# wo loaded behind the last feed-forward weights, its low parts on VectorE, the first chunk's loads in written order, later x by the sync queue

## The chip, the cores and the metric

The kernel runs on one core of a Trainium2 chip. The metric is the device time of one execution in microseconds (us), as the median of several runs. The work is shared by TensorE (PE: matrix multiplications), VectorE (DVE), ScalarE (ACT), GpSimd (POOL) and the sync engine (SP), which only issues transfers (DMAs). ACT issues some transfers too. Each engine works through its own list of instructions in order, and an instruction that waits for another engine or for a transfer holds up all that stands behind it on its engine.

## What is computed

One sequence of 2048 tokens with 512 features. The layer-normalised input goes two ways: through an attention of 32 heads of 16 features, in which each token sees 8 earlier ones, two apart, and through a feed-forward net of 1792 hidden units with a squared ReLU. The result is the input plus the attention's output times the SiLU of the feed-forward's output.

```python
xn = _layernorm(x)
# attention
q, k, v = (xn @ wqkv) split into 32 heads of 16
idx = pos[:, None] - (arange(8) * 2)[None, :]      # masked where idx < 0
logits = einsum("bhsd,bhswd->bhsw", q, k[idx]) * 0.25
s = einsum("bhsw,bhswd->bhsd", softmax(logits), v[idx]) @ wo
# feed-forward
h = relu(xn @ w1 + b1) ** 2
g = silu(h @ w2 + b2)
return x + s * g
```

## The kernel before

**Number format.** Every matrix product is made of three passes: each float32 operand is split into a high part (a copy rounded to the format that TensorE reads, by `high`, on ACT) and a low part (what the rounding left, by `low`, a subtraction). `PASSES` multiplies high by high, high by low and low by high.

**Stages.** The tokens are 16 tiles of 128. The first stage normalises and transposes the tiles and makes q, k and v, which go to DRAM in head order (`sq`, `sk`, `sv`). The transposed tiles of later chunks are stored too (`sx`). The second stage is the feed-forward net and the output product, in four chunks `c` of 512 tokens. In each chunk the loop over `f`, the 14 blocks of 128 hidden units, calls `up(c, f)` (12 matmuls into a PSUM tile `ph`) and, two blocks behind, `down` (12 matmuls that add to four PSUM tiles `pb`). Blocks 0 and 1 of a chunk are computed at the end of the stage before it. `out_product(t)` multiplies tile t of the attention's output with `wot`, the split wo.

**ph and its two buffers.** The `ph` tiles share two PSUM buffers, so `up(0, f)` writes where `up(0, f - 2)` wrote. In chunk 0, for f from 2 to 11, ACT makes the ReLU, the high part of its square and the square itself, all out of `ph` and the last one back into `ph`, and `lowh(f)` on VectorE subtracts the high part: only then is the buffer free. For other f and in later chunks GpSimd subtracts from a copy in SBUF.

**Attention on VectorE.** The attention is a generator, `attention`, over 8 units of 256 tokens: per unit four times a product and a reduction for the logits (`pr`, then `L`), a softmax, and four times a product and a reduction for the output (`pv`, then `v`), which `store` writes to `so`. Its instructions are placed between the others by a planner: `clock` holds a running estimate of TensorE's and of VectorE's time, and `pump(margin)` emits attention work as long as VectorE's estimate stays below TensorE's plus the margin. `load` asks for k, q and v of a unit: `defer` holds the issue (by ACT) until TensorE's estimate has reached a due time, which is VectorE's estimate plus `FREE` (2000 ns). `start` notes when the data should be there (`LOAD`, 10500 ns later), and the planner places no work on it before.

**Weights.** `load_w(f)` loads a raw block of w1 and of w2 into two of four buffers (tag `z`), and `next_w` splits the next block (high on ACT, low on GpSimd) and asks for the block two further on. In the loop of chunk 0, step f splits block f + 3 and asks for block f + 5, so that step 8 asks for the last, block 13. wo is loaded raw at steps 3 and 6 (`rwo`, two tiles, four transfers of 32 partitions each) and split at steps 6 to 9, its low parts on GpSimd. `load_o` loads a unit of the attention's output (`oq`), `trans_o` transposes it on VectorE and copies the high part on ACT, `lowo` makes the low part, `load_r` loads rows of x for the residual, `finish` multiplies, adds and stores.

**Order.** Compute instructions keep the order in which the program writes them (`keep_in_program_order`). Of the transfers that SP issues, those through `queue` keep it among themselves; those through `dma` are put where a scheduler finds it best. The chunk's transposed x (`load_xT`, tile `xU`) is issued by ACT, behind `up(c, 13)` of the chunk before.

Of the kernel before, what the change touches and what calls it, by code (L numbers as in the profile page):

```python
# [9 lines left out]
F32 = mybir.dt.float32  # L10
# [5 lines left out]
P = 128  # L16
S = 2048
D = 512
# [15 lines left out]
BI = 16  # L34
# [18 lines left out]

MATMUL, VMATMUL, TRANSPOSE, DVE_FIXED, SHARED, SLACK, LATE, ROOM0, ROOM = 227, 120, 150, 150, 200, 500, 3000, 500, 3500

BEHIND, FAR, FREE, LAND, LOAD = 5000, 9000, 2000, 4500, 10500


@with_exitstack
def body(ctx: ExitStack, tc: tile.TileContext, x, wqkv, wo, w1, b1, w2, b2, out):  # L60
# [3 lines left out]
    clock = {"PE": 0.0, "V": 0.0}  # L64
# [30 lines left out]
    PE, V, A, G = Ordered(nc.tensor, "PE"), Ordered(nc.vector, "V"), Ordered(nc.scalar), Ordered(nc.gpsimd)  # L95
# [4 lines left out]
    dma = nc.sync.dma_start  # L100

    def queue(out, in_):

        tc.keep_in_program_order(dma(out, in_))
# [16 lines left out]
    def psT(name):  # L121
        return psum.tile([P, 512], F32, name=name, tag="tp", bufs=2)
# [4 lines left out]
    def high(hi, lo, src):  # L127
        A.activation(hi, src, AF.Copy)

    def low(hi, lo, src, eng):  # L130
        eng.tensor_sub(lo, src, hi.bitcast(F32))

    def split(hi, lo, src, eng):
        high(hi, lo, src)
        low(hi, lo, src, eng)
# [13 lines left out]
    def tile_rows(a, t):  # L149
        return a[t // 2 * UP:(t // 2 + 1) * UP, :].rearrange("(p e) d -> e p d", e=2)[t % 2]  # L150
# [109 lines left out]
    def attention():  # L260
# [74 lines left out]
        def store(u):  # L335
            v = tiles.pop(("v", u))
            row = so[0, u * UP:u * UP + 1, :]
            dst = bass.AP(tensor=row.tensor, offset=row.offset, ap=[[BI * CH, NB], [S * CH, GR], [1, BI * CH]])
            dma(dst, v[:, :BI, :].rearrange("p i c -> p (i c)"))
            done_units[0] = u + 1  # L340

        def load(u, names):
            if u == NU:
                return
            for n in names:
                while done_tiles[n][0] < 2 * (u + 1):
                    yield None
                t = max(clock["V"] + FREE if u else 0, done_tiles[n][1][u] + LAND)
                if u == 1 and n != "v" and n not in released:
                    held[n] = partial(start, n, u)  # L350
                else:
                    defer(t, partial(start, n, u))
# [47 lines left out]

    def load_w(f):
        r1, r2 = (piece(f"{n}{f}") for n in ("w1r", "w2r"))
        send = queue if f < 2 else dma
        send(r1.rearrange("p (k c) -> p k c", c=P), w1[:, f * P:(f + 1) * P].rearrange("(k p) c -> p k c", p=P))
        send(r2, w2[f * P:(f + 1) * P, :])
        raws[f] = r1, r2

    def next_w():
# [186 lines left out]
    def load_xT(c):  # L595
        xT[c] = xTa.tile([P, KT, TPC, 2, P], FR, name=f"xU{c}", tag="xT")
        for kt in range(KT):
            A.dma_start(xT[c][:, kt].bitcast(F32), sx[c][:, kt])

    hs = {}  # L600

# [21 lines left out]
    def lowh(f):  # L623
        h, ph, t = hs[f]
        if ph is not None:
            not_before(t)
            V.tensor_sub(h[:, 1], ph, h[:, 0].bitcast(F32))
# [282 lines left out]
    oqs, oTs = {}, {}  # L910

    def load_o(u, force):

        if u in oqs or (done_units[0] <= u and not force):
            return
        while done_units[0] <= u:
            flush(None)
            pump(clock["V"] - clock["PE"] + 4000)
        oqs[u] = p2.tile([P, UP // 64, 2, 2, CH], F32, name=f"oq{u}", tag="oq")
        for g in range(GR):  # L920
            src = so[g, u * UP:(u + 1) * UP, :].rearrange("(b p e) c -> p b (e c)", p=32, e=2)
            dma(oqs[u][32 * (g // 2):32 * (g // 2) + 32, :, g % 2].rearrange("p b e c -> p b (e c)"), src)

    def trans_o(t, pT):
        src = pT.rearrange("p (g n) -> p g n", g=4)
# [11 lines left out]
    def out_product(t, ps, cols=slice(0, D)):  # L937
        o = oTs[t]
        n = 0
        for g in range(4):  # L940
            for a, b in PASSES:
                PE.matmul(ps[:, cols], o[:, a, g], wot[:, b, g, cols], start=n == 0, stop=n == 11)
                n += 1
        pws[t] = ps
# [6 lines left out]

    def load_r(t):
        xrs[t] = p2.tile([P, D], F32, name=f"xr{t}", tag="xr", bufs=2)
        dma(xrs[t], tile_rows(x, t))

    def finish(t, eng, xt=None, cols=slice(0, D)):
        z = gs[t // TPC, t % TPC]
# [9 lines left out]
    for c in range(NCH):  # L967
        last = c == NCH - 1
        if c == 0:
            for j in range(TPC):  # L970
                begin(c, j)
        pb = [pbs[c, j] for j in range(TPC)]
        t0 = c * TPC
        room = ROOM if c else ROOM0
        for f in range(2, NF):
            up(c, f)
            if c == 0:
                next_w()
            pump()
            if c == 0 and f in (3, 6):  # L980

                i = f // 6
                rwo[i] = p2.tile([P, 2, D], F32, name=f"rwo{i}", tag="oT", bufs=2)
                for q in range(4):
                    rows = wo[q * P + 64 * i:q * P + 64 * i + 64, :].rearrange("(g p) n -> p g n", g=2)
                    dma(rwo[i][32 * q:32 * q + 32], rows)
            if c == 0:
                if 6 <= f < 10:
                    split(wot[:, 0, f - 6], wot[:, 1, f - 6], rwo[(f - 6) // 2][:, (f - 6) % 2], G)
            elif f == 2:  # L990
                finish(t0 - 4, G)
            elif f == 3:
                finish(t0 - 3, G)
                load_r(t0 - 2)
                load_r(t0 - 1)
                trans_o(t0 - 2, psT(f"pT{t0 - 2}"))
                trans_o(t0 - 1, psT(f"pT{t0 - 1}"))
            elif f == 4:
                lowo(t0 - 2)
                lowo(t0 - 1)  # L1000
            elif f == 5:
                out_product(t0 - 2, psT(f"pw{t0 - 2}"))
            elif f == 6:
                finish(t0 - 2, G)
                out_product(t0 - 1, psT(f"pw{t0 - 1}"))
            elif f == 7:
                finish(t0 - 1, G)
            if f == 2 and c:
                load_o(c * 2 - 1, True)
            elif f >= 7:  # L1010
                load_o(c * 2, f >= 9)
            if f in (9, 10) and not last:
                load_r(t0 + f - 9)
            if f == 10:
                for i in range(2):
                    trans_o(t0 + i, psT(f"pT{t0 + i}"))
            if f == 11:
                for i in range(2):
                    lowo(t0 + i)
            if f == 11 or (last and f > 11):  # L1020
                load_o(c * 2 + 1, f > 12)
            downs = [f - 2]
            if last and f == NF - 1:
                downs = []
            elif not last and f > NF - 3:
                downs = [f - 3, f - 2] if f == NF - 1 else []
            for i in downs:
                for j in range(TPC):
                    down(pb, i, j)
            pump(room)  # L1030
            lowh(f)
        out_product(t0, psT(f"pw{t0}"))
        if last:
            out_product(t0 + 1, psT(f"pw{t0 + 1}"))
        pump(room)
        if not last:
            for j in range(TPC):
                for i in range(2):
                    down(pb, NF - 2 + i, j)
                pump(room if j < 2 else -SLACK)  # L1040
                gate(c, j, pb)
                begin(c + 1, j)
            for i in range(2):
                up(c + 1, i)
                pump(ROOM)
                lowh(i)
                load_o(c * 2 + 1, False)
            out_product(t0 + 1, psT(f"pw{t0 + 1}"))
            pump(ROOM)
        else:  # L1050
            for i in range(2, TPC):
                trans_o(t0 + i, psH(f"pT{t0 + i}"))
            for i in range(2, TPC):
                lowo(t0 + i)
            xl = xTa.tile([P, TPC, 512], F32, name="xlast", tag="xT")
            dma(xl.rearrange("p (h e) n -> p h (e n)", e=2),
                x[t0 * P:(t0 + TPC) * P, :].rearrange("(h p e) n -> p h (e n)", p=P, e=2))
            for j in range(TPC):
                for f in range(NF - 3, NF):
                    down(pb, f, j)  # L1060
                gate(c, j, pb)
                if j < 2:
                    finish(t0 + j, V, xl[:, j])
            for j in range(2, TPC):
                n = D // 2 if j == TPC - 1 else D
                for i in range(0, D, n):
                    cols = slice(i, i + n)
                    out_product(t0 + j, (psT if i else psH)(f"pw{t0 + j}_{i}"), cols)
                    finish(t0 + j, V, xl[:, j], cols)
# [21 lines left out]
```

## Time and profile before

| | |
|---|---|
| median of 3 runs | 486.02 us (485.04 to 487.2) |
| the profiled execution | 485.13 us, its span 483.1 us |
| TensorE busy | 477.4 us, 99% of the span |
| VectorE, ScalarE, GpSimd busy | 423.0, 240.0, 225.3 us |
| transfers | 81.47 MB, mean 169 GB/s |

The profile is of one execution. Its times count from the first instruction of the span. "PEld" is the loading of weights into TensorE, which overlaps the multiplications. Rows of the timeline merge like instructions that follow each other without a gap: start, duration, engine, source line, operation, tiles written and read, shapes, count, and in brackets the idle time before the row and what ended it. Almost all compute rows carry the line of one helper (L91), so tiles tell what a row is. An engine name with a q is its instruction queue issuing a transfer. Of the DMA queues, q1 holds the transfers that SP issues and q10 those that ACT issues; both use the same 16 DMA engines.

### The profile page before, as it was taken

Reading aid. Unit: us, or ns where it says so; the run is one execution under the profiler, and the core shown is the slowest. Engines: PE = TensorE matmul, PEld = TensorE weight load, DVE = VectorE, ACT = ScalarE, POOL = GpSimd, SP = SyncE. Lnnn points to the kernel's source line nnn. Section 1 sums busy time; section 2 is a strip of 40 time slices with the busy share of each in tenths; the row PEclk is TensorE's granted clock in tenths of the full one; section 3 lists DMA queues with packets and bytes.
Section 4 is the critical chain, followed back from the end, with each engine's and each line's share of the span. In section 5 each row is a group of like instructions: output and inputs, shape, how many; then the busy total and the mean of one; then the engine's idle time right before and its main releaser. Section 6 shows DMA issues by size and latency. Waiting matters only on the chain.

```text
span 483.1 us, 6128 instructions
## 1 busy us (share of the span) xinstructions
PE 477.4 (99%) x2190; PEld 396.6 (82%) x2190; DVE 423.0 (88%) x352; ACT 240.0 (50%) x441; POOL 225.3 (47%) x178
## 2 busy tenths in 40 slices
PE   8999999999999999999999999999999999999996
PEld 5888888888888888888888888888888888888885
DVE  5978999899499899999999999999999999889133
ACT  5548798856566565273513345342234543423240
POOL 1459853116986699436543322434433345253210
PEclk9999999999999999999999999999999999999999
DMA  7899999998779996571627548071707725220321
GB/s 283 243 251 258 277 243 302 263 306 269 209 198 228 255 224 151 178 166 43 170 72 185 115 164 190 26 189 43 197 16 196 224 48 145 43 86 27 87 105 71
DMA packets 71002, 81.47 MB, mean 169 GB/s; under 512 B 6204, under 2 KB 55612, under 8 KB 70972
## 3 DMA queue, kind: packets, MB, share of 16 engines
q1 hardware_dynamic: 65788, 54.87, 41.3%
q10 hardware_dynamic: 5184, 26.22, 21.8%
q8 instruction: 17, 0.28, 0.2%
q14 instruction: 13, 0.11, 0.1%
HBM read 50.60 MB, written 27.32 MB: 161 GB/s over the span
## 4 chain that ended last, share of the span: by engine, by line
PE 98%; DMA 1%; DVE 0%; POOL 0%; issue 0%; ACT 0%; POOLq 0%
PE ph L91 32%; PE pb L91 32%; PE pm L91 12%; PE pq L91 9%; PE pw L91 9%; PE pv L91 4%; DMA x<-in_A_x 1%; PE pxT L91 0%; DVE z L91 0%; DVE st L91 0%; POOL rs L91 0%; DVE xn L91 0%; ACT xT0f L91 0%; DVE mv L91 0%; DVE rs L91 0%
## 5 line engine op out<-in xcount | busy, mean ns | idle before, releaser
L91 PE MATMUL pb<-w,h 128*128 128x512 f32 x672 | 160.1, 389 | 0.0
L91 PEld LDWEIGHTS pb<-w,h 128*128 128x128 f32 x672 | 126.1, 188 | 26.2
L91 POOL TENSOR_TENSOR h<-hf,h 128x512 fp32r<-128x512 f32 x46 | 67.7, 1473 | 157.5 <-ACT hf L91 157.5
L91 PE MATMUL ph<-xU,w 128*128 128x512 f32 x504 | 120.2, 389 | 0.0
L91 ACT ACTIVATE ph<-ph,b1t 128x512 f32<-128x512 f32 x56 | 37.0, 661 | 153.9 <-PE ph L91 144.0
L91 PEld LDWEIGHTS ph<-xU,w 128*128 128x128 f32 x504 | 94.6, 188 | 19.6
L91 DVE TENSOR_TENSOR pr<-k,q 128x2048 f32<-128x2048 f32 x32 | 78.7, 2460 | 3.2 <-DMA q<-sq 2.5
L91 DVE TENSOR_TENSOR pv<-v,L 128x2048 f32<-128x2048 f32 x32 | 77.3, 2417 | 3.8 <-POOL L L91 3.1
L91 DVE TENSOR_REDUCE L<-pr 128x128 f32<-128x2048 f32 x32 | 73.0, 2281 | 0.7
L91 DVE TENSOR_REDUCE v<-pv 128x256 f32<-128x2048 f32 x32 | 72.9, 2279 | 0.7
L91 PE MATMUL pw<-wot,oT 128*128 128x512 f32 (+1 forms) x204 | 45.9, 376 | 0.0
L91 PEld LDWEIGHTS pw<-wot,oT 128*128 128x128 f32 x204 | 36.8, 188 | 7.1
L91 POOL TENSOR_TENSOR w<-w1r,w 128x512 fp32r<-128x512 f32 x14 | 31.6, 2259 | 23.4 <-ACT w L91 23.2
L91 PE MATMUL ph<-xT,w 128*128 128x512 f32 x168 | 40.0, 389 | 0.0
L91 PEld LDWEIGHTS ph<-xT,w 128*128 128x128 f32 x168 | 31.5, 188 | 6.6
L91 PE MATMUL pm<-wq,S 128*128 128x512 f32 x144 | 36.8, 392 | 0.0
L91 ACT ACTIVATE h<-ph 128x512 fp32r<-128x512 f32 x56 | 33.5, 599 | 1.8
L91 PE MATMUL pq<-wq,xT 128*128 128x512 f32 x132 | 30.9, 393 | 0.0
L91 PEld LDWEIGHTS pm<-wq,S 128*128 128x128 f32 x144 | 26.2, 188 | 5.3 <-DVE S L91 0.4
L91 PEld LDWEIGHTS pq<-wq,xT 128*128 128x128 f32 x132 | 24.5, 188 | 5.9 <-ACT xT L91 0.7
L91 ACT ACTIVATE hf<-ph 128x512 f32<-128x512 f32 x46 | 27.4, 595 | 1.9 <-POOL h L91 1.9
L91 PE MATMUL pm<-wq,xt 128*128 128x512 f32 x108 | 27.6, 392 | 0.0
(96 smaller groups left out, 531.0 us busy)
## 6 DMA issues: line engine op xcount, KB each, us to landing
k<-sk ACTq DMA_DIRECT2D x8, 960.0 KB, 7.1
v<-sv ACTq DMA_DIRECT2D x8, 960.0 KB, 7.4
sx<-xt SPq DMA_DIRECT2D x12, 512.0 KB, 5.8
xU<-sx ACTq DMA_DIRECT2D x12, 512.0 KB, 5.9
x<-in_A_x SPq DMA_DIRECT2D x16, 256.0 KB, 6.4
sk<-stg SPq DMA_DIRECT2D x8, 512.0 KB, 4.3
sq<-stg SPq DMA_DIRECT2D x8, 512.0 KB, 7.5
sv<-stg SPq DMA_DIRECT2D x8, 512.0 KB, 5.0
```

The source lines that it names most:

```text
L91: return tc.keep_in_program_order(f(*a, **k))
```

## The change

Seven edits. `load_w` always uses `queue`. `load_xT` goes through `queue`, so by SP, not ACT. Of unit 0 and tiles 0 and 1, the store of the attention's output and the loads of `load_o` and `load_r` go through `queue`. The due time of a load of v is 9000 ns (`STORED`) behind VectorE's estimate, where it was 2000. wo is asked for at steps 8 and 9 in place of 3 and 6, each half in two transfers that fill all 128 partitions, where it took four of 32 partitions. Its high parts are made at steps 10 and 11, two at a step, and its low parts on VectorE at the ends of these steps, behind `lowh`, where GpSimd made them at steps 6 to 9. In chunk 0, `load_o(0)` is asked for from step 9 (forced from step 10), `trans_o` of tiles 0 and 1 comes at step 12 in place of 10, and `lowo` at 13 in place of 11.

```diff
-BEHIND, FAR, FREE, LAND, LOAD = 5000, 9000, 2000, 4500, 10500
+BEHIND, FAR, FREE, STORED, LAND, LOAD = 5000, 9000, 2000, 9000, 4500, 10500
...
-            dma(dst, v[:, :BI, :].rearrange("p i c -> p (i c)"))
+            (dma if u else queue)(dst, v[:, :BI, :].rearrange("p i c -> p (i c)"))
...
-                t = max(clock["V"] + FREE if u else 0, done_tiles[n][1][u] + LAND)
+                t = max(clock["V"] + (STORED if n == "v" else FREE) if u else 0, done_tiles[n][1][u] + LAND)
...
-        send = queue if f < 2 else dma
-        send(r1.rearrange("p (k c) -> p k c", c=P), w1[:, f * P:(f + 1) * P].rearrange("(k p) c -> p k c", p=P))
-        send(r2, w2[f * P:(f + 1) * P, :])
+        queue(r1.rearrange("p (k c) -> p k c", c=P), w1[:, f * P:(f + 1) * P].rearrange("(k p) c -> p k c", p=P))
+        queue(r2, w2[f * P:(f + 1) * P, :])
...
-            A.dma_start(xT[c][:, kt].bitcast(F32), sx[c][:, kt])
+            queue(xT[c][:, kt].bitcast(F32), sx[c][:, kt])
...
-            dma(oqs[u][32 * (g // 2):32 * (g // 2) + 32, :, g % 2].rearrange("p b e c -> p b (e c)"), src)
+            (dma if u else queue)(oqs[u][32 * (g // 2):32 * (g // 2) + 32, :, g % 2].rearrange("p b e c -> p b (e c)"), src)
...
-        dma(xrs[t], tile_rows(x, t))
+        (dma if t > 1 else queue)(xrs[t], tile_rows(x, t))
...
-            if c == 0 and f in (3, 6):
-
-                i = f // 6
+            if c == 0 and f in (8, 9):
+
+                i = f - 8
                 rwo[i] = p2.tile([P, 2, D], F32, name=f"rwo{i}", tag="oT", bufs=2)
-                for q in range(4):
-                    rows = wo[q * P + 64 * i:q * P + 64 * i + 64, :].rearrange("(g p) n -> p g n", g=2)
-                    dma(rwo[i][32 * q:32 * q + 32], rows)
+                for g in range(2):
+                    row = wo[64 * i + 32 * g:64 * i + 32 * g + 1, :]
+                    queue(rwo[i][:, g], bass.AP(tensor=row.tensor, offset=row.offset, ap=[[P * D, 4], [D, 32], [1, D]]))
             if c == 0:
-                if 6 <= f < 10:
-                    split(wot[:, 0, f - 6], wot[:, 1, f - 6], rwo[(f - 6) // 2][:, (f - 6) % 2], G)
+                if f in (10, 11):
+                    for g in range(2):
+                        high(wot[:, 0, 2 * (f - 10) + g], None, rwo[f - 10][:, g])
...
-            elif f >= 7:
-                load_o(c * 2, f >= 9)
+            elif f >= (7 if c else 9):
+                load_o(c * 2, f >= (9 if c else 10))
...
-            if f == 10:
+            if f == (10 if c else 12):
                 for i in range(2):
                     trans_o(t0 + i, psT(f"pT{t0 + i}"))
-            if f == 11:
+            if f == (11 if c else 13):
                 for i in range(2):
                     lowo(t0 + i)
...
             lowh(f)
+            if c == 0 and f in (10, 11):
+                for g in range(2):
+                    low(wot[:, 0, 2 * (f - 10) + g], wot[:, 1, 2 * (f - 10) + g], rwo[f - 10][:, g], V)
```

An access pattern such as `[[P * D, 4], [D, 32], [1, D]]` lists step and count of each dimension, the outermost first: here 4 groups of 32 rows of 512 elements, read into 128 partitions.

## The prediction, made before the result was known

> **What bounds the kernel now.** I read the page first: the engines' shares, then the chain of work that ended last.
>
> ```profile
> PE 477.4 (99%) x2190; PEld 396.6 (82%) x2190; DVE 423.0 (88%) x352; ACT 240.0 (50%) x441; POOL 225.3 (47%) x178
> PE 98%; DMA 1%; DVE 0%; POOL 0%; issue 0%; ACT 0%; POOLq 0%
> ```
>
> TensorE is the chain. Whether it has anything to lose is read from its timeline around the change.
>
> ```profile
> 185.19 2.88 PE L91 MATMUL ph<-xT,w 128*128 128x512 f32 x12
> 190.63 5.60 PE L91 MATMUL ph<-xT,w 128*128 128x512 f32 x24
> ...
> 201.51 2.88 PE L91 MATMUL pw<-wot,oT 128*128 128x512 f32 x12
> ...
> 296.71 5.60 PE L91 MATMUL ph<-xU,w 128*128 128x512 f32 x24
> ```
>
> From 185.19 to 190.63 stand 12 matmuls of `up` and 12 of `down`: 0.227 us each, 2.72 for 12. Row after row follows without a gap (from 190.63 to 201.51 are 48). The change leaves the matmuls and their order as they are, so in this stretch nothing can be gained; time can only be lost where an operand or a PSUM buffer is late. So I look for the smallest margin. It lies where two `up` follow each other, in the row of 24 at 190.63: its second half, `up(0, 13)`, starts at 190.63 + 2.72 = 193.35 and writes the buffer of `up(0, 11)`, which VectorE must have left.
>
> ```profile
> 183.68 0.68 DVE L91 TENSOR_TENSOR h<-ph,h 128x512 fp32r<-128x512 f32 x1
> 184.28 1.30 DVE L91 STREAM_TRANSPOSE pT<-oq 128x512 f32<-128x512 f32 x2
> 185.50 2.24 DVE L91 TENSOR_REDUCE v<-pv 128x256 f32<-128x2048 f32 x1
> 187.67 0.67 DVE L91 TENSOR_TENSOR h<-ph,h 128x512 fp32r<-128x512 f32 x1
> 188.26 1.27 DVE L91 TENSOR_TENSOR oT<-pT,oT 128x512 fp32r<-128x512 f32 x2
> 189.46 2.42 DVE L91 TENSOR_TENSOR pv<-v,L 128x2048 f32<-128x2048 f32 x1
> 191.80 0.68 DVE L91 TENSOR_TENSOR h<-ph,h 128x512 fp32r<-128x512 f32 x1
> ```
>
> The `h` rows are `lowh(9)`, `lowh(10)` and `lowh(11)`. The last ends at 192.48: 0.87 us of margin. VectorE has no gap, so whatever is put ahead of `lowh(11)` and waits comes out of that.
>
> **The change, part by part.**
>
> *Low parts of wo on VectorE.* Two subtractions (128x512, 0.6 us apart as in the `oT` pair, 1.27 for two) now stand between `lowh(10)` and `lowh(11)`. Two transposes (1.30) and two `lowo` (1.27) leave their places ahead of them. By the planner's margins the stretch becomes: `v` reduction, `pv` product, `lowh(10)`, two subtractions, `v` reduction, `lowh(11)`. After 184.36 that is 2.24 + 2.42 + 0.67 + 1.27 + 2.28 + 0.68, less some 0.1 overlap each: about 193.4 where 192.48 was. A wait of VectorE for q earlier on, next to the old wo loads, should shrink:
>
> ```profile
> 158.43 2.29 DVE L91 TENSOR_TENSOR pr<-k,q 128x2048 f32<-128x2048 f32 x1 [2.46 <-DMA q<-sq]
> ```
>
> With 1 to 2 us of it gone `lowh(11)` ends at 191.4 to 192.4. So the subtractions cost nothing, as long as they don't wait.
>
> *wo's new place.* They wait for ACT's high parts, and these for the loads. On SP the loads now stand behind block 13:
>
> ```profile
> 180.38 0.33 SPq L405 DMA_DIRECT2D w2r<-in_B_w  x1
> 183.38 0.53 ACTq L91 DMA_DIRECT2D k<-sk  x1
> ```
>
> ```profile
> 179.06 1.29 POOL L91 TENSOR_TENSOR w<-w2r,w 128x512 fp32r<-128x512 f32 x1
> ```
>
> SP issues block 13's w2 when GpSimd is through with block 11 (179.06 + 1.29 = 180.35). GpSimd was held by the landing of earlier blocks, behind the old wo loads, so this may come up to 2 us sooner: 178.5 to 180.4. wo follows 0.4 us later, its bytes about 1.3 us after that and behind w2's: start at 180.2 to 182.4; I take 181.3.
>
> How fast it comes depends on how many DMA engines it gets. The list of transfers answers:
>
> ```profile
> DMA packets 71002, 81.47 MB, mean 169 GB/s; under 512 B 6204, under 2 KB 55612, under 8 KB 70972
> k<-sk ACTq DMA_DIRECT2D x8, 960.0 KB, 7.1
> ...
> sk<-zero SPq DMA_DIRECT2D x1, 28.0 KB
> sv<-zero SPq DMA_DIRECT2D x1, 28.0 KB
> b1t<-in_B_b SPq DMA_DIRECT2D x1, 7.0 KB, 7.6
> ```
>
> Its 25 rows, of which the first and the last three stand here, add up to 262 transfers. Of the 6204 packets under 512 bytes, 1792 are b1t's 4-byte elements (7 KB) and 224 the 256-byte rows of the two fills (28 KB each). That leaves 4188 = 16 x 262 - 4: one small closing packet for each engine and transfer, but four fewer. All transfers have an outermost count that 16 divides (128, 32 or 16), except the two fills, with 14. So I read it as 16 engines each, and 14 for a fill: the outermost count limits the engines. The new wo loads read with an outermost count of 4 (the old had 32), and I take 4 engines. The fills have 14 on both sides, while wo's target has 128, so this isn't proved. The Trainium skill (DMA: Bandwidth & Descriptors, "Why a DMA increments its semaphore by 16 and not by 1") says that the largest number up to 16 is taken that divides both sides' slowest counts: here 4. By that rule the sum is the one below, by the target's 128 alone it would be nothing.
>
> A full set of engines and the competition of ACT's queue:
>
> ```profile
> DMA packets 216, 0.38 MB, mean 379 GB/s; under 512 B 19, under 2 KB 35, under 8 KB 216
> ...
> q10 hardware_dynamic: 70, 0.54, 104.5%
> q1 hardware_dynamic: 8, 0.00, 1.1%
> ...
> q1 hardware_dynamic: 74, 0.12, 20.9%
> ...
> q10 hardware_dynamic: 282, 1.50, 96.6%
> ```
>
> These are four stretches: 178.5 to 179.5, SP's weights alone, 379 GB/s; 165.5 to 168 and 149 to 152, beside a load of v and of k by ACT, where SP's transfers got 1.1% and 20.9%; and 184.7 to 191.5, k and q of unit 3, which fill all engines (96.6%). Four engines move 379 / 4 = 95 GB/s, so the first half of wo (524 KB) takes 5.5 us. From 181.3 to 184.7 it gets 3.4 of them; 2.1 are left. Until 191.5 it gets 1 to 21% of 6.8 us, 0.1 to 1.4. The rest ends at 192.2 to 193.5: landing L = 193.
>
> From L: one high part, 0.6, two subtractions, 1.3, the reduction, 2.3, `lowh(11)`, 0.7: L + 4.9 = 197.9 against 193.35. **The loss is 4.5 us.** With the early start (180.2), 4.5 us come before 184.7 and the last 1.0 at 21% by 189.6: a loss of 1.1. With the late one (182.4) 3.2 us are left at 191.5, and a 195.5 gives 7.0. While ACT waits, ReLU and squares of block 11 stand behind it, but they need L + 3.0, less than VectorE's path. Late next is wo's second half, at L + 5.5, then `oq`, queued behind it: high parts, subtractions, transposes, ACT's copies and `lowo` end at about L + 11; `out_product(0)` moves with TensorE to 201.51 + 4.5 = 206.0 = L + 13. No second stall.
>
> *Later x by SP.* Transfers and their wait (the end of `up(c, 13)`) stay; only the issuing queue changes.
>
> ```profile
> 283.31 1.78 ACTq L91 DMA_DIRECT2D xU<-sx  x4
> 288.82 0.52 SPq L339 DMA_DIRECT2D so<-v  x1
> ```
>
> ```profile
> xU<-sx ACTq DMA_DIRECT2D x12, 512.0 KB, 5.9
> ```
>
> Issued until 285.1, landed 5.9 later, wanted at 296.71: 5.7 us to spare, and SP's next, the store, stands behind it. ACT saves 1.8 us of issuing three times, off the path. I cost it at nothing; if SP were held by that store first, the last transfer would go out at 290.7 and land at 296.6, with a later VectorE up to 3 us too late.
>
> *v asked for 7 us later.* ACT loses an idle wait, here the longest:
>
> ```profile
> 208.60 1.28 ACT L91 ACT_TABLE_LOAD   x1 [8.71 <-DMA so<-v]
> ```
>
> TensorE didn't stand for it. In return v comes 7 us later, while between a store and the next product with v lie four logits products and reductions (19 us) against 9 + 10.5 us that the planner reckons; a few units may slip by 1 or 2 us. The end bears that:
>
> ```profile
> 447.06 0.52 SPq L339 DMA_DIRECT2D so<-v  x1
> 456.48 0.73 DVE L91 STREAM_TRANSPOSE pT<-oq 128x512 f32<-128x512 f32 x1 [8.26 <-ACT hf L91]
> 473.51 5.75 PE L91 MATMUL pw<-wot,oT 128*128 128x512 f32 x36
> ```
>
> The last store is out at 447.06, and its transposes, held by a PSUM buffer, run at 456.48 for the product at 473.51. With 0.73, a copy and a subtraction in between, some 12 us are free: nothing, or 1 to 3 us if the slip went over that.
>
> *Written order* of the other loads: SP already issued them in this order; nothing.
>
> **Sum.** 485.13 (span 483.1 and 2.0 around it) + 4.5 = 489.6. The median of the runs lies 0.9 above the profiled execution, so 490.5 by runs; I take the middle, 490.0.
>
> **The rivals.**
>
> A. *wo is there in time*, because 128 target partitions spread it over 16 engines: 1 MB at 379 GB/s takes 2.8 us, from 181.3 to 184.1, ahead of k. Then L + 4.9 is earlier than 192.4, and the time stays at 485.1 to 486.0: not slower. For it: no transfer of before has a different count on its two sides with one of them under 16. Against it: the fills. It decides where L falls below 188.45. A softer form (0.05 of A's chance) has 4 engines, but an even sharing with ACT's queue: the 2.1 us would take 4.2, L = 188.9, loss 0.5; the 1.1% beside 104.5% speaks against it. The Trainium skill (DMA: Bandwidth & Descriptors, "Issuing engines are not separate DMA queues") says that transfers of all issuers run on the same engines and interleave, which is this form.
>
> B. *SP is held when x is wanted*, or attention slips past its slack: 1 to 3 us, 487 to 489. Against it: the order and the margins above.
>
> C. *Faster.* wo's old loads gone from beside q, k and the weights could give ACT and GpSimd air; but TensorE has no gap in this stretch for it to fill. By the rows under 0.5 us; more only by something that they don't show.
>
> **How the numbers follow.** Forecast (4 engines, L past 188.45) 0.66, A 0.24, B 0.07, C 0.03. The forecast's own range is 486 to 493: losses of 1.1 to 7.0 on 485.1 to 486.0. With A the range is 485.0 to 493. A difference under 0.5% (2.4 us) can't be told from none: slower takes 0.61 of the forecast and 0.06 of B, together 0.67; the same takes A's 0.24, the forecast's small losses, 0.05, and 0.01 each of B and C, together 0.31; faster is C's other 0.02.
>
> **What would show it.** Right: a gap on TensorE of 3 to 7 us ahead of the last 12 of 24 `ph` rows near 193, ended by VectorE's `h`; ahead of that, VectorE idle at `wot`, ACT idle at `wot` for `rwo`; `rwo` landing 10 us or more after its issue. Wrong: `rwo` landing in under 6 us and TensorE without a gap (A); a gap ahead of `ph<-xU` (B). A gap nowhere but a changed time would leave my whole reading in doubt.

## The result, and the profile after

| | before | after |
|---|---|---|
| median (6 runs each) | 486.41 us (484.97 to 487.2) | 493.27 us (491.84 to 494.42) |
| ratio after / before | | 1.0144, 95% interval 1.0124 to 1.0164 |
| profiled execution, its span | 485.13, 483.1 us | 494.42, 492.6 us |

The change makes the kernel slower by 1.4%, 6.9 us between the medians. The prediction had the sign right and was 3.3 us too low (490.0, range to 493.0).

The page of the changed kernel comes first: the busy time of TensorE, the granted clock in 40 slices, and the chain of work that ended last by engine.

```profile
PE 482.1 (98%) x2190; PEld 399.3 (81%) x2190; DVE 424.5 (86%) x356; ACT 241.2 (49%) x441; POOL 228.0 (46%) x174
...
PEclk9999999999999999799999999999999999999999
...
PE 94%; DMA 2%; SPq 1%; DVE 1%; issue 1%; ACT 0%; POOL 0%; ACTq 0%; DVEq 0%; POOLq 0%
```

TensorE was 98% of the chain and is 94%. In one slice, the 17th of the 40 (197 to 209 us), the granted clock falls to 7 tenths. So there is one place to look at. The timeline there (start, duration, engine, operation, tiles, count; in brackets the idle time before the row and what ended it):

```profile
187.11 2.88 PE L91 MATMUL ph<-xT,w 128*128 128x512 f32 x12
...
192.55 2.88 PE L91 MATMUL ph<-xT,w 128*128 128x512 f32 x12
194.11 0.53 ACTq L91 DMA_DIRECT2D k<-sk  x1
...
194.79 0.52 ACTq L91 DMA_DIRECT2D q<-sq  x1
195.64 1.15 ACT L91 ACTIVATE wot<-rwo 128x512 fp32r<-128x512 f32 x2 [8.20 <-DMA oq<-so]
196.30 1.29 DVE L91 TENSOR_TENSOR wot<-rwo,wot 128x512 fp32r<-128x512 f32 x2 [8.40 <-ACT wot L91]
...
197.51 2.28 DVE L91 TENSOR_REDUCE v<-pv 128x256 f32<-128x2048 f32 x1
...
199.71 0.68 DVE L91 TENSOR_TENSOR h<-ph,h 128x512 fp32r<-128x512 f32 x1
...
200.44 5.24 PE L91 MATMUL ph<-xT,w 128*128 128x512 f32 x12 [5.01 <-DVE h L91]
...
211.00 2.88 PE L91 MATMUL pw<-wot,oT 128*128 128x512 f32 x12
```

Read it from below. TensorE stands 5.01 us ahead of `up(0, 13)`, the second half of what was one row of 24 matmuls before, because `lowh(11)` (199.71) is late. `lowh(11)` stands on VectorE behind the two subtractions of wo and a reduction; the subtractions waited 8.40 us for ACT's high parts; these began at 195.64, and the row says that ACT had stood idle for 8.20 us until a transfer of `oq` landed. That is odd: the high parts read `rwo`, not `oq`. Between the two stand the issues of k and q of unit 3, at 194.11 and 194.79, where the kernel before issued k at 183.38. The chain of waits runs the same way (start, duration, what):

```profile
182.13 1.83 SPq L104
...
185.28 9.48 DMA oq<-so
194.77 0.02 issue
194.79 0.52 ACTq L91
195.31 0.33 issue
195.64 0.64 ACT wot L91
```

A transfer of `oq` took 9.48 us, and what it released was ACT's issue of q. Last, the granted clock (stretch: length, busy time of TensorE and instructions, granted clock, share of the DMA engines, GB/s):

```profile
195.30:198.40 3.10, 0.13 (x1) 1.00 0.90 201
198.40:200.40 2.00, 0.00 (x0) 0.51 1.02 237
200.40:205.30 4.90, 4.86 (x12) 0.50 0.83 193
205.30:208.00 2.70, 2.70 (x13) 1.00 0.38 85
```

About 3 us after TensorE fell idle its clock was halved, and it stayed so for 4.9 us after TensorE had resumed: the 12 matmuls of `up(0, 13)` came every 427 ns, not every 227. So the place costs twice: 5.17 us of standing (start to start, beyond the 227 ns) and 12 times 0.2 = 2.40 of slow matmuls, 7.57 together. The spans of the two profiled executions differ by 9.5. The other 1.9 lie ahead of all this: the row at 187.11 is the one at 185.19 before. They come from the first 20 us, whose loads vary from run to run (the first experiment, with the same beginning, has the same row at 185.09). From 211.00 to the last output product, 483.00 (473.51 before), nothing more is lost.

**What oq has to do with k.** The program's listing gives for every instruction the counters that it waits for. A transfer counts its completion on one of eight counters, DMAHW0 to DMAHW7, which SP's and ACT's transfers take in turn, and it is not issued until the transfer that had the counter before has landed:

```
SP   DMA rwo0<-wo  (no. 1)                      its counter: DMAHW5
...
SP   DMA oq0<-so   (no. 1)  [waits DMAHW1]
SP   DMA oq0<-so   (no. 4)  [waits DMAHW4]
...
ACT  DMA k3<-sk             [waits DMAHW1]
ACT  DMA q3<-sq             [waits DMAHW4]
ACT  ACTIVATE wot<-rwo0     [waits DMAHW5]
```

So k follows `oq`'s first transfer on its counter, and q its fourth. The trace has each increment of these counters:

| transfer | increments from DMA engines | last one | 
|---|---|---|
| wo 1, 2, 3, 4 | 4 each | 184.57, 188.11, 190.95, 193.73 |
| oq 1 | 12, then 4 | 186.12, then 194.08 |
| oq 4 | 12, then 4 | 187.83, then 194.77 |

wo's counters have one more increment each, 0.9 to 1.5 us after the issue and so well ahead of the landing; the table leaves it out.

wo's transfers ran on four engines. Those of `oq` ran on 16: twelve had done their part by 186 to 188, and the other four, with all of wo queued ahead, 8 and 7 us later. k went out 0.03 us after `oq`'s first transfer had landed, q 0.02 us after the fourth. wo's first half, for which all seemed to wait, had been there since 188.11.

### The profile page after: what moved, and what is told of

It is laid out like the page before. It is cut to its first block, busy times and chain, and to the rows that moved or that the text cites. A ratio compares the mean times of both kernels' runs of the same rounds, so it can differ in the third digit from the quotient of the medians.

```text
span 492.6 us, 6128 instructions
## 1 busy us (share of the span) xinstructions
PE 482.1 (98%) x2190; PEld 399.3 (81%) x2190; DVE 424.5 (86%) x356; ACT 241.2 (49%) x441; POOL 228.0 (46%) x174
## 2 busy tenths in 40 slices
DMA packets 70890, 81.47 MB, mean 165 GB/s; under 512 B 6092, under 2 KB 55500, under 8 KB 70860
## 4 chain that ended last, share of the span: by engine, by line
PE 94%; DMA 2%; SPq 1%; DVE 1%; issue 1%; ACT 0%; POOL 0%; ACTq 0%; DVEq 0%; POOLq 0%
PE ph L91 30%; PE pb L91 29%; PE pm L91 12%; PE pq L91 9%; PE pw L91 9%; PE pv L91 4%; DMA oq<-so 2%; SPq L104 1%; DMA x<-in_A_x 1%; PE pxT L91 0%; DVE v L91 0%; DVE z L91 0%; DVE wot L91 0%; DVE st L91 0%; DVE h L91 0%
## 5 line engine op out<-in xcount | busy, mean ns | idle before, releaser
L91 POOL TENSOR_TENSOR h<-hf,h 128x512 fp32r<-128x512 f32 x46 | 82.8, 1801 | 121.3 <-ACT hf L91 121.2
L91 DVE TENSOR_TENSOR pr<-k,q 128x2048 f32<-128x2048 f32 x32 | 77.3, 2416 | 0.8
L91 PE MATMUL ph<-xT,w 128*128 128x512 f32 x168 | 42.5, 405 | 5.0 <-DVE h L91 5.0
L91 PEld LDWEIGHTS ph<-xT,w 128*128 128x128 f32 x168 | 33.1, 198 | 12.5 <-DVE h L91 5.4
L91 POOL TENSOR_TENSOR w<-w1r,w 128x512 fp32r<-128x512 f32 x14 | 24.2, 1727 | 32.5 <-ACT w L91 32.4
L91 POOL TENSOR_TENSOR L<-L,sm_None 128x512 f32<-128x512 f32 x7 | 13.2, 1893 | 31.5 <-DVE sm_None L91 21.0
```

Source lines behind the costliest of these rows:

```text
L91: return tc.keep_in_program_order(f(*a, **k))
```

## The experiments

Theory T, from the above: four engines hold wo, `oq` stands behind wo on these four, k and q share counters with `oq`, and ACT, with wo's high parts and the ReLU of block 11 behind these issues, is held until 194.8. The rivals: P, the prediction's own (wo's landing itself is late, starved by k and q), and V (the place of the low parts on VectorE costs by itself). TensorE's gap and its clock are compared, since the beginning of a run varies by some 2 us.

**wo on 16 engines.** The old access pattern at the new place.

```diff
-for g in range(2):
-    row = wo[64 * i + 32 * g:64 * i + 32 * g + 1, :]
-    queue(rwo[i][:, g], bass.AP(tensor=row.tensor, offset=row.offset, ap=[[P * D, 4], [D, 32], [1, D]]))
+for q in range(4):
+    rows = wo[q * P + 64 * i:q * P + 64 * i + 64, :].rearrange("(g p) n -> p g n", g=2)
+    queue(rwo[i][32 * q:32 * q + 32], rows)
```

> The changed kernel, with one thing undone: wo comes in four transfers of 32 partitions per tile, as before the change, instead of two with an outermost count of 4; the queue, the time and the low parts on VectorE stay as changed. Theory T (ScalarE is held at the issue of k and q of unit 3, because their completion counters are shared with the loads of oq, and these lie behind wo on four DMA engines): wo takes under 4 us, oq lands before 190, ScalarE is not held, TensorE has no gap at the last 12 of 24 ph rows near 195, the granted clock stays up; 485 to 486 us, some 7.5 below the changed kernel. Theory P (as predicted: wo's own landing is what is late): the same here. Theory V (the place of the low parts on VectorE ahead of lowh(11) is what costs): the gap of 5 us stays, 492 to 494.

Median 484.88 us of 11 runs against 485.44 of 15 of the kernel before; ratio 0.999, 95% interval 0.9975 to 1.0005. The loss is gone. Its timeline:

```profile
183.28 0.52 ACTq L91 DMA_DIRECT2D k<-sk  x1
...
185.31 1.14 ACT L91 ACTIVATE wot<-rwo 128x512 fp32r<-128x512 f32 x2
...
190.53 5.60 PE L91 MATMUL ph<-xT,w 128*128 128x512 f32 x24
191.27 0.67 DVE L91 TENSOR_TENSOR h<-ph,h 128x512 fp32r<-128x512 f32 x1
```

k goes out at 183.28, the high parts follow, and the 24 `ph` matmuls run through. V falls: `lowh(11)` ends at 191.94, ahead of `up(0, 13)` at 190.53 + 2.72 = 193.25. T and P both fit. With more transfers the counters fell otherwise too (here q follows wo's second transfer), so that this run alone doesn't say which of the links was cut.

**As many transfers, on four engines.** Each row of wo in two halves, eight transfers in all.

```diff
-    row = wo[64 * i + 32 * g:64 * i + 32 * g + 1, :]
-    queue(rwo[i][:, g], bass.AP(tensor=row.tensor, offset=row.offset, ap=[[P * D, 4], [D, 32], [1, D]]))
+    for h in range(0, D, D // 2):
+        row = wo[64 * i + 32 * g:64 * i + 32 * g + 1, h:h + D // 2]
+        queue(rwo[i][:, g, h:h + D // 2],
+              bass.AP(tensor=row.tensor, offset=row.offset, ap=[[P * D, 4], [D, 32], [1, D // 2]]))
```

> Beside the kernel with 32-partition transfers: wo in as many transfers (eight) but each on an outermost count of 4, packets of 1024 bytes. If the number of transfers is what counts, the gap goes and the time is 485 to 486. If the four engines are, as theories T and P say, wo again takes 10 us or more and the gap is 5 us or more: 492 to 496.

492.39 us, and the gap again:

```profile
199.13 4.64 PE L91 MATMUL ph<-xT,w 128*128 128x512 f32 x12 [5.78 <-DVE h L91]
```

What counts is the four engines, not the number of transfers. With eight of them k follows wo's eighth transfer on its counter: this landed at 192.15, and k went out at 192.17.

**Nothing of wo ahead of lowh(11).** High and low parts two blocks later, the low ones ahead of `trans_o`.

```diff
-if f in (10, 11):
-    for g in range(2):
-        high(wot[:, 0, 2 * (f - 10) + g], None, rwo[f - 10][:, g])
+if f == 12:
+    for g in range(4):
+        high(wot[:, 0, g], None, rwo[g // 2][:, g % 2])
...
+if c == 0 and f == 12:
+    for g in range(4):
+        low(wot[:, 0, g], wot[:, 1, g], rwo[g // 2][:, g % 2], V)
...
-if c == 0 and f in (10, 11):
-    for g in range(2):
-        low(wot[:, 0, 2 * (f - 10) + g], wot[:, 1, 2 * (f - 10) + g], rwo[f - 10][:, g], V)
```

> The changed kernel, with wo's high parts and low parts moved two blocks later (to f = 12, ahead of the transposes of oq), so that nothing of wo stands ahead of lowh(11) on ScalarE or VectorE; wo's transfers, oq and k and q of unit 3 stay. Theory T: ScalarE is still held at the issue of k and q until about 195, relu(11) behind it, lowh(11) some 2 us later: a gap of 2 to 3 us at the same matmuls. Theories P and V: nothing that lowh(11) needs waits for wo any more, no gap.

489.74 us:

```profile
192.97 0.53 ACTq L91 DMA_DIRECT2D q<-sq  x1
193.88 0.66 ACT L91 ACTIVATE ph<-ph,b1t 128x512 f32<-128x512 f32 x1 [8.53 <-PE ph L91]
195.70 0.69 DVE L91 TENSOR_TENSOR h<-ph,h 128x512 fp32r<-128x512 f32 x1 [4.89 <-ACT ph L91]
...
196.44 4.60 PE L91 MATMUL ph<-xT,w 128*128 128x512 f32 x12 [3.09 <-DVE h L91]
```

Now the ReLU is first behind q's issue. The row names TensorE as what it waited for, but TensorE had long been done: it was q's issue, 0.9 us ahead. The gap is 3.09, where P and V had none. P falls here.

**k and q later.** One number in the planner; wo still by four engines.

```diff
+if u == 3 and n != "v":
+    t += 11000
```

> The changed kernel, with k and q of unit 3 asked for 11 us later and nothing else touched: on ScalarE their issue now stands behind wo's high parts. wo still comes by four engines. Theory T: ScalarE is not held ahead of wot, its high parts run when wo lands (188 to 191), lowh(11) is in time, no gap at the last 12 ph rows: 485 to 487, but for what the later k and q cost. Theories P and V: the gap of 4 to 5 us stays.

485.29 us, no gap:

```profile
187.78 0.63 ACT L91 ACTIVATE wot<-rwo 128x512 fp32r<-128x512 f32 x1 [1.39 <-DMA rwo<-in_A_wo]
...
190.98 5.60 PE L91 MATMUL ph<-xT,w 128*128 128x512 f32 x24
...
193.32 0.63 ACT L91 ACTIVATE wot<-rwo 128x512 fp32r<-128x512 f32 x1 [2.02 <-DMA rwo<-in_A_wo]
...
194.02 0.53 ACTq L91 DMA_DIRECT2D k<-sk  x1
```

ACT now waits for `rwo` itself, 1.39 and 2.02 us, and that costs nothing. wo on four engines is late for nobody; only the transfer issues ahead of its high parts were.

**oq behind k and q.** `load_o(0)`, issued by ACT, at f = 11, and the residual tiles at 11 and 12 in place of 9 and 10, so that k and q follow no unfinished transfer.

```diff
-            (dma if u else queue)(oqs[u][32 * (g // 2):32 * (g // 2) + 32, :, g % 2].rearrange("p b e c -> p b (e c)"), src)
+            (dma if u else A.dma_start)(oqs[u][32 * (g // 2):32 * (g // 2) + 32, :, g % 2].rearrange("p b e c -> p b (e c)"), src)
...
-elif f >= (7 if c else 9):
-    load_o(c * 2, f >= (9 if c else 10))
+elif f >= (7 if c else 11):
+    load_o(c * 2, f >= (9 if c else 11))
...
```

> The changed kernel, with the loads of oq and of the first two residual tiles moved from f = 9 to f = 11, behind k and q of unit 3 (oq issued by ScalarE). wo still comes by four engines, but k and q share no completion counter with an unfinished transfer, so they go out near 185 and run beside wo: this is the meeting of transfers that the prediction reckoned with. If k and q starve wo, as the prediction had it, the first half of wo lands at 192 to 193.5 and TensorE stands 4 to 5 us at the last 12 ph rows. If they do not, it lands near 188 and the gap there is 0 to 1 us. If ScalarE is held by full engines and not by a counter, it stands at the issue of k all the same, until 190 or later. oq comes late in any case, so a gap of 1 to 5 us at out_product may follow; the total is not what this run is for.

497.71 us. The gap moved:

```profile
183.71 0.52 ACTq L91 DMA_DIRECT2D k<-sk  x1
...
187.49 0.63 ACT L91 ACTIVATE wot<-rwo 128x512 fp32r<-128x512 f32 x1 [1.13 <-DMA rwo<-in_A_wo]
...
190.96 5.60 PE L91 MATMUL ph<-xT,w 128*128 128x512 f32 x24
...
195.20 0.63 ACT L91 ACTIVATE wot<-rwo 128x512 fp32r<-128x512 f32 x1 [4.44 <-DMA rwo<-in_A_wo]
...
199.48 0.63 ACT L91 ACTIVATE wot<-rwo 128x512 fp32r<-128x512 f32 x1 [3.64 <-DMA rwo<-in_A_wo]
...
212.01 2.50 PE L91 MATMUL pw<-wot,oT 128*128 128x512 f32 x5 [10.01 <-DVE oT L91]
```

ACT isn't held: k goes out at 183.71. `up(0, 13)` follows without a gap, since wo's first half had landed at 187.47. The starvation that the prediction reckoned with is real, but it strikes the second half: its two transfers landed at 195.18 and 199.45, some 16 and 20 us after their issue, against 10 and 13 in the changed kernel. With `oq` late as well, `out_product(0)` waits 10.01.

**Half of oq later.** The sharpest test of the counters: four of `oq`'s loads stay, the other four go behind k and q, at f = 12 by ACT, the residual tiles at f = 12 and 13. By the listing k now follows wo's second transfer, q its third.

```diff
+part_o(u, range(GR if u else GR // 2), dma if u else queue)
...
+if c == 0 and f == 12:
+    part_o(0, range(GR // 2, GR), A.dma_start)
...
```

`part_o` is the loop of `load_o` over a part of the eight loads.

> The changed kernel, with four of the eight loads of oq left where they are and the other four, with the residual tiles, moved behind k and q of unit 3 (issued by ScalarE). wo and half of oq still queue on the four engines as before. By the program's listing the completion counters have moved: k now follows wo's second transfer on its counter and q wo's third (188.1 and 190.9 in the changed kernel), not oq's first and fourth (194.1 and 194.8). Theory T: ScalarE issues k when wo's second transfer lands, near 188, and q at its third, 191 to 193; from q's issue to TensorE's resumption it took 5.65 us, so a gap of 1 to 3.5 us at the 12 ph matmuls in place of 5.2. If full engines or ACT's own ring hold ScalarE, it stays until 194 or later and the gap is 5 us or more. oq is late in any case, so a gap at out_product may follow; the total is not what this run is for.

```profile
186.74 0.52 ACTq L91 DMA_DIRECT2D k<-sk  x1
189.71 0.52 ACTq L91 DMA_DIRECT2D q<-sq  x1
190.56 1.15 ACT L91 ACTIVATE wot<-rwo 128x512 fp32r<-128x512 f32 x2 [4.93 <-DMA rwo<-in_A_wo]
...
195.37 3.02 PE L91 MATMUL ph<-xT,w 128*128 128x512 f32 x12 [1.74 <-DVE h L91]
...
208.88 3.42 PE L91 MATMUL pw<-wot,oT 128*128 128x512 f32 x8 [5.06 <-DVE oT L91]
```

wo's second transfer landed at 186.72 and its third at 189.69: each issue comes 0.02 us later. `up(0, 13)` starts 5.66 us after q's issue (5.65 in the changed kernel), so the gap is 1.74. Neither full engines nor ACT's own queue held it. (493.75 us, the late `oq` costing 5.06 at `out_product`.)

**The four engines alone, in the kernel before.** wo at its old steps 3 and 6, low parts on GpSimd, only the access pattern new.

```diff
-for q in range(4):
-    rows = wo[q * P + 64 * i:q * P + 64 * i + 64, :].rearrange("(g p) n -> p g n", g=2)
-    dma(rwo[i][32 * q:32 * q + 32], rows)
+for g in range(2):
+    row = wo[64 * i + 32 * g:64 * i + 32 * g + 1, :]
+    dma(rwo[i][:, g], bass.AP(tensor=row.tensor, offset=row.offset, ap=[[P * D, 4], [D, 32], [1, D]]))
```

> The kernel before, with one part of the change alone: wo in two transfers per tile with an outermost count of 4, at the old places (f = 3 and 6), low parts on GpSimd. wo then takes 10 us or more per half beside the loads, but is wanted only later. If the four engines cost only where something waits behind them, TensorE has a gap of 0 to 1 us: 485 to 487. If they hold up SyncE's weights behind them, w4 to w8 come late: a gap of 2 to 6 us near 140 to 180, 487 to 493.

494.45 us against 485.06 of the kernel before beside it: as slow as the whole change, at another place:

```profile
158.64 0.52 ACTq L91 DMA_DIRECT2D q<-sq  x1
159.27 0.66 ACT L91 ACTIVATE ph<-ph,b1t 128x512 f32<-128x512 f32 x1 [11.95 <-DMA rwo<-in_A_wo]
...
161.88 4.45 PE L91 MATMUL ph<-xT,w 128*128 128x512 f32 x12 [3.85 <-DVE h L91]
...
167.84 2.29 DVE L91 TENSOR_TENSOR pr<-k,q 128x2048 f32<-128x2048 f32 x1 [3.91 <-DMA q<-sq]
...
170.79 3.01 PE L91 MATMUL ph<-xT,w 128*128 128x512 f32 x12 [1.55 <-DVE h L91]
```

I had expected late weights. They do come late (ACT waits 5.10 and 3.10 us for `w1r`), but both large gaps of TensorE are the same hold as above: q of unit 2 follows wo's second transfer on its counter, this landed at 158.62, and ACT, with a ReLU behind the issue, had stood for 11.95 us. The second gap, at 170.79, comes from the same q: VectorE's product at 167.84 waited 3.91 us for it to land, with `h` behind it. After that TensorE loses 0.1 to 0.3 us a block up to 194, to which the late weights may add. So the old place wouldn't have saved the change; the access pattern is its cost.

**The later v, and x by ACT.** On the kernel with 16 engines, one edit in each of two runs:

```diff
-BEHIND, FAR, FREE, STORED, LAND, LOAD = 5000, 9000, 2000, 9000, 4500, 10500
+BEHIND, FAR, FREE, STORED, LAND, LOAD = 5000, 9000, 2000, 2000, 4500, 10500
...
-            queue(xT[c][:, kt].bitcast(F32), sx[c][:, kt])
+            A.dma_start(xT[c][:, kt].bitcast(F32), sx[c][:, kt])
```

> The kernel with wo in 32-partition transfers, and v asked for 2 us behind the clock as before the change, not 9. ScalarE's idle wait for the store of v (8.7 us near 208.6 in the kernel before) comes back. As predicted, the later v is worth nothing on TensorE: no gap, 484.5 to 486.5. If the changed order on ScalarE needs it, a gap of 1 us or more near 190 to 215, or time slipping by 1 to 3 us.

> The kernel with wo in 32-partition transfers, and the later x issued by ScalarE again, as before the change. As predicted, who issues it is worth nothing: 484.5 to 486.5, no gap at the first matmuls that read xU near 297, 354 and 411; x lands 6 us after its issue, against 8 by SyncE. If x by SyncE had eaten time somewhere, this run is lower by it.

485.35 and 485.38 us, neither with a gap. ACT's wait for the store of v comes back, shorter, and TensorE doesn't feel it (4.96 us at 212.43). x lands 5.9 us after ACT's issue as before, 7.3 after SP's in the run with 16 engines. So neither edit is worth anything that these single runs can tell from noise.

**Filling the wait.** Is the halved clock a consequence of standing, or of something else at that time? 20 added matmuls (4.5 us), written at the head of step 13 with the tile taken there, at step 13 with the tile taken at step 12, and at step 12 ahead of `trans_o` (the edit, shortened):

```diff
+fill = psT("fill")
+for n in range(20):
+    matmul(fill, w12[0][:, 0, 1, :P], w12[0][:, 0, 1, :], start=n == 0, stop=n == 19)
```

> The changed kernel with 20 more matmuls of 227 ns (4.5 us) into a spare PSUM tile, whose result is not used, in the place where TensorE stands idle for 5.0 us; all that the wait hangs on is untouched. If the halved clock behind the gap (0.5 from 198.4 to 205.3) comes from TensorE's having been idle, the granted clock stays at 1.0, the 12 matmuls behind the gap take 227 ns and not 427, and TensorE's whole excess there falls from 7.6 to 5.0 to 5.5 us: 490 to 492. If the clock drops for another reason (the load on the chip at that time), it drops here too: 493 to 495.

> As the first try to fill the wait, but the spare PSUM tile is taken ahead of the transposes of oq, so that the 20 added matmuls (4.5 us, result not used) wait for nothing and run where TensorE stands idle for 5 us. If the halved clock comes from TensorE's having been idle, the granted clock stays at 1.0 there, the 12 ph matmuls behind the gap take 227 ns and not 427, and TensorE's excess at the place, without the fill, falls from 7.6 to some 5 us: 490 to 492. If the clock drops for another reason, it drops here too: 493 to 495.

> As the two tries before it, with the 20 added matmuls (4.5 us, result not used) written before the transposes of oq in the program, so that they stand on TensorE right behind the last full block of ph (0, 12) and wait for nothing. If the halved clock comes from TensorE's having been idle, the granted clock stays at 1.0 there, the 12 ph matmuls behind the gap take 227 ns and not 427, and TensorE's excess at the place falls from 7.6 to some 5 us: 490 to 492. If the clock drops for another reason, it drops here too: 493 to 495.

The first two tries missed: the spare tile took a PSUM buffer of the transposes of `oq` and waited 9.17 and 8.22 us for it (500.10 and 500.05 us), so they only lengthened the gap. The third, written ahead of the transposes, fits:

```profile
193.95 4.69 PE L1017 MATMUL fill<-w 128*128 128x512 f32 x20
199.49 3.03 PE L91 MATMUL ph<-xT,w 128*128 128x512 f32 x12 [0.84 <-DVE h L91]
```

And the stretch behind the gap (columns as above: the granted clock stands behind the count):

```profile
199.50:202.30 2.80, 2.80 (x12) 1.00 1.05 253
```

ACT is held as before (q at 193.81), yet the clock stays at 1.00 and the 12 matmuls are fast. 4.53 of filling and 1.15 of rest make 5.69 us where the changed kernel loses 7.57; 491.19 us, for more work.

The other runs say the same, each gap by its row above and the granted clock behind it:

| gap, us | 0.84 | 1.55 | 1.74 | 3.09 | 3.85 | 5.01 | 5.06 | 5.78 | 10.01 |
|---|---|---|---|---|---|---|---|---|---|
| clock in the 2.7 to 4.9 us behind | 1.00 | 1.00 | 1.00 | 0.57 | 0.65 | 0.50 | 0.50 | 0.55 | 0.50 |
| half clock in all, us | 0 | 0 | 0 | 3.41 | 3.41 | 6.83 | 3.41 | 6.83 | 10.24 |

The gaps lie between 158 and 212 us and beside quite different transfers; what goes with the loss of clock is the gap's length. The last row is the whole time at half clock that the trace records, gap included. Values like 0.57 are means: the clock is 0.50 or 1.00, and a part of the stretch was at each.

## Why the prediction was right or wrong

- **TensorE without a gap, smallest margin at `up(0, 13)`: right.** The loss came exactly there, ended by VectorE's `h`, with VectorE idle at `wot` and ACT idle ahead of `wot`, as written. Two signs differed: ACT's wait ended with `oq`, not `rwo`, and wo's first half landed 5.4 and 8.3 us after its issues, not 10 or more.
- **Low parts on VectorE cost nothing by themselves: right.** 1.3 us of margin are left with wo in time (16 engines). VectorE's wait of 2.46 us for q is gone, as expected.
- **wo on four engines: right.** The wo transfers show four increments each, and 6204 small packets became 6092: 8 x 16 closing packets less, 4 x 4 more. The page's count of packets, then the stretch from 182 to 184.4, where wo's transfers are alone: 99 GB/s (last column), against 95 reckoned.

```profile
DMA packets 70890, 81.47 MB, mean 165 GB/s; under 512 B 6092, under 2 KB 55500, under 8 KB 70860
```

```profile
182.00:184.40 2.40, 2.40 (x13) 1.97 (x12) 2.40 (x2) 0.00 (x0) 2.40 (x3) 1.00 0.26 99
```

  The Trainium skill's rule (DMA: Bandwidth & Descriptors, "Why a DMA increments its semaphore by 16 and not by 1"), the largest number up to 16 that divides both sides' slowest counts, held here with 4 at the source and 128 at the target.
- **The start of wo at 181.3 (180.2 to 182.4): wrong, too late.** SP issued wo from 179.13, and measured against TensorE, which was 1.9 us later in that run, at 177.2. The sum has the issue 1.3 us ahead of the start, at 178.9 to 181.1. I had allowed 2 us for the old wo loads' being gone from the weights' way; they gave 3.6 (block 13's w2 at 178.74 - 1.92, where it was 180.38).
- **"k and q of unit 3 by ACT at 184.7 to 191.5 starve it", L = 193: the step that failed.** The competition didn't take place, because k and q were not issued. I treated ACT's issues as given by the trace of before and asked only what they do to wo; I didn't ask what has to be finished before ACT may issue them, and whether wo holds that up. L was 188.11, or 186.2 measured against TensorE. By the prediction's own rule, which put the turning point at 188.45, that would have been no loss. Nor would the competition have brought one: where k and q did run beside wo (the run with `oq` behind k and q), its first half landed at 187.47 and `up(0, 13)` followed without a gap. In place of the starved wo stood ACT's hold, until q's issue at 194.79. ACT began on `wot` at 195.64, 193.7 measured against TensorE; that this lies near the 193 reckoned for another reason is luck, and so are the right sign and the stall of about the right size.
- **The size of the stall, 4.5: near, 5.0 by the row.** The path behind ACT was worked out rightly, L + 4.9 to the end of `lowh(11)`: from ACT's start on `wot` at 195.64 to TensorE's 200.44 it is 4.80. Only that start hung on q's issue. The upper end of the range has a slip: in the late case 3.2 us of wo are left at 191.5, so it lands at 194.7, for a loss of 6.2; the 195.5 and the 7.0 don't follow.
- **A term was missing: the slow matmuls behind the gap, 2.4 us.** It is what lifts the result over the range. The Trainium skill says that gaps on TensorE beyond some 3 us bring half its clock (TensorE: Matmul & The Clock Gate, "Why this matters for your kernels"); the table above agrees, with 1.74 harmless and 3.09 not. With a forecast gap of 4.5 the term belonged in the sum: 489.6 + 2.4 = 492.0 on the profiled execution, 492.9 by runs.
- **No second stall: right.** From 211.00 on the distances are those of before.
- **Later x by SP, v asked for later: right,** each undone alone without effect, in the kernel with 16 engines. The last product still starts without a gap: its operand is ready at 475.67 + 0.69 = 476.36, for 483.00.
- **Written order worth nothing: open.** It puts all of `oq` right behind wo, a link of the chain that was found; it wasn't undone alone, and with wo on 16 engines it costs nothing.
- **The rivals.** A (wo in time) had the right consequence: with 16 engines the change is level with before. Its softer form, even sharing with ACT's queue, is seen where k and q ran beside wo. For the first half it came out milder still: wo's second transfer landed 4.22 us behind its first, against 3.54 in the changed kernel. For the second half it was harder than even: SP's queue moved 0.12 MB between 188 and 191 and 0.06 MB between 191 and 195, 40 and 15 GB/s, against the 99 of wo alone. B didn't occur. C neither: the four kernels without the stall (16 engines, the same with v or x undone, k and q later) take 484.9 to 485.4, and the kernel before, beside them, 485.0 to 485.4.

## What to carry to other kernels

Put a large count outermost in a transfer's access pattern: an outermost 4 made not only this transfer about four times slower (99 GB/s, against 379 on all engines) but held the last shares of every transfer queued behind it. When a transfer becomes slow, look up which transfers take over its completion counter, or that of one queued behind it, and which compute instructions stand behind their issue: an engine that both computes and issues can be held by data that it never reads. And count a stall of TensorE of 3 us or more at its length plus 1.5 to 2.4 us of half clock; one of 1.74 us cost no clock here.

## What the runs showed of the hardware that I had not expected

- A transfer on 16 engines is done when its last share is: `oq`'s first had 12 shares done by 186.12 and the last four at 194.08, because of another transfer's queue on four engines.
- An issue waits, by a wait that stands in the program, for the transfer that used its completion counter before, even one by another engine and with other data: for k and q, landing and issue lie 0.02 to 0.03 us apart in eleven cases of six kernels. SP is held in the same way: in the changed kernel `oq`'s last three loads go out at 188.13, 190.97 and 193.75, each 0.02 us behind wo's second, third and fourth transfer.
- TensorE's clock changes in steps of 3.41 us: in every trace here it keeps a value for a multiple of that (3.41, 6.83 or 10.24 us at half) until the last piece, which the end cuts. So where a gap lies on these steps counts too. The clock fell 3.0 us into the gap of 5.01 (at 198.44) and 2.4 us into that of 5.78, but 0.4 us after the end of that of 3.09 (1.00 up to 196.80, 0.50 up to 200.21, 1.00 behind) and 1.2 us after the end of that of 3.85. The slow matmuls cost 2.4 us behind the gap of 5.01, 1.5 behind that of 5.06, 1.7 behind that of 3.09 and 2.2 behind that of 10.01: no order by length.
